# A new hand-written order for the first two batches of a fused attention and feed-forward kernel

## The chip, the cores and the metric

The kernel runs on one core of a Trainium2 chip. The metric is the device time of one execution in microseconds (us). In the text PE is the matrix engine, DVE the vector engine, ACT the activation engine, POOL the general engine that also issues "software" DMAs, SP the engine that only issues DMAs. PEld is PE's weight load. Each engine works through its own list in order and waits on semaphores for the others.

## The reference

Cosine attention over 8 batches of 12 heads (448 positions, 64 wide), then a two-layer feed-forward net with exact gelu on the 3584 tokens:

```
q_n = q / (norm(q) + 1e-6);  k_n = k / (norm(k) + 1e-6)
attn = softmax(q_n @ k_n.T / tau)
x = (attn @ v) as (3584, 768)
out = gelu(x @ w_in) @ w_out        # w_in 768 x 2048, w_out 2048 x 768
```

Input and output are float32; the matrix products run in bfloat16.

## The kernel before

Four heads form a quad; a batch has three quads, so there are 24, numbered 0 to 23. Quad 0 is handled as two halves (units 0 and 1), every other quad as one unit (unit u is quad u - 1). For each unit: Q and K are loaded (`load_qk`, SP's queue), squared (`square`) and summed (`reduce`, DVE), the norm is made as exp(0.5 ln) on ACT (`logs`, `roots`) and inverted on DVE (`inverses`), Q and K are multiplied by it (`scale`), transposed (`transposes`: on PE through a PSUM bank and a DVE copy, `copies`, or by a DMA on SP's queue). The first argument of `transposes`, `copies`, `scale`, `square` and `reduce` is a unit, that of `scores`, `exps`, `sums`, `values` and `normalise` a quad. `scores` writes a pair of PSUM banks, of which there are two (st0, st1), `exps` is one ACT instruction over such a pair. `sums` and `values` are products with ones and with V, `turned`, `inverted`, `spread` and `normalise` (DVE) divide by the sums and write x.

The feed-forward part of a batch: 96 products `mm` for 16 blocks of 128 columns (`hp`), a gelu for each (ACT), then "pieces" of the second layer (`op`), each of 16 steps `run(1)` of four instructions over 64x64 tiles; a piece ends in a reduce on DVE, or a copy on ACT and an add on DVE. The pieces of a batch run in the next batch's attention; two pairs of banks serve them in turn.

V and both weights are loaded by POOL (`load_v`, `load_wi`, `load_wo`), converted to bfloat16 on the way. W_in comes in four parts, W_out in four; `load_wi(3)` holds the upper half of the columns for the last third of x.

The first two batches are written out as a list in the function `opening()`; the place of a call in this list is the place of its instructions in its engine's own list. From batch 2's feed-forward on, loops (`attention`, `first`) make the order. Q and K live in four buffers in turn (`qkp`). `spin` is an idle product on constants, to keep PE busy at the start. `table` loads ACT's function table: one set has exp and logarithm, the other gelu. Norm inputs that are ready together share one `logs` and `roots`: the list `groups` says which units; each has a constant tile (`root2`) for its root:

```
groups = [[n] for n in range(NQ + 2)] + [[NQ + 2, NQ + 3], [2 * NQ + 1], [2 * NQ + 2]]
sr_t[n] = root2[2 if len(groups[n]) == 2 else n % 2][:, :math.prod(shapes[n])]
```

Of the kernel before, what the change touches and what calls it, by code (L numbers as in the profile page):

```python
# [9 lines left out]
F32 = mybir.dt.float32  # L10
# [6 lines left out]
def kernel(  # L17
# [73 lines left out]
    root2 += [consts.tile([128, 8 * C, 2], F32, name=f"root4_{n}") for n in range(1)]  # L91
    for t in root2:
        nc.vector.memset(t[:, :, 1], 1e-6)
# [33 lines left out]
    def load_qk(g, queue=None):  # L127
        b, n = divmod(g, NQ)
        t = qkp.tile([128, 2, 2, C, D], F32, tag="qk", name=f"qk{g}")
        qk_t[g] = t  # L130
        for s0, s1 in ((0, 1), (1, 2)) if g == 0 else ((0, 2),):
            for i, src in enumerate((q, k)):
# [4 lines left out]
                        "(s h) (p c) d -> (h p) s (c d)", h=2, c=C))  # L137

# [341 lines left out]
    def upto(f, n, last=None):  # L480
        last = {load_qk: NG, load_v: NV, root: len(groups), load_wi: NQ + 1, load_wo: 4}.get(f, NU)
# [56 lines left out]
    def opening():  # L538
        load_qk(0)
        table(EXP_SET)  # L540
        load_qk(1)
        load_qk(2)
        spin(20)
        late_copy()
        load_qk(3)
        x_t[0] = xp.tile([128, KD, S], BF16, tag="x", name="x0")
        square(0, ((AC, Q),))
        square(0, ((AC, K),))
        reduce(0, Q)
        reduce(0, K)  # L550
        square(1, ((AC, Q),))
        load_v(0)
        logs(0)
        reduce(1, Q)
        roots(0)
        load_wi(0)
        square(1, ((AC, K),))
        inverses(0)
        square(2, ((AC, Q),))
        reduce(1, K)  # L560
        scale(0, ((GP, 1),))
        logs(1)
        reduce(2, Q)
        roots(1)
        scale(0, ((GP, 0),))
        spin(2)
        transposes(0, 1)
        square(2, ((AC, K),))
        inverses(1)
        spin(1)  # L570
        transposes(0, 0)
        square(3, ((AC, Q),))
        copies(0, 1)
        scale(1, ((GP, 0),))
        copies(0, 0)
        square(3, ((AC, K),))
        scale(1, ((GP, 1),))
        load_qk(4)
        spin(1)
        transposes(1, 0)  # L580
        reduce(2, K)
        scores(0, ((0, 0), (0, 1)))
        load_v(1)
        transposes(1, 1)
        copies(1, 0)
        logs(2)
        scores(0, ((0, 2), (0, 3)))
        roots(2)
        load_wi(1)
        exps(0, ((0, 0), (0, 1)))  # L590
# [638 lines left out]
    def attention(b, fill):  # L1229
# [12 lines left out]
        def inverted_norms():  # L1242
            if 2 * b + 6 < len(groups):
                inverses(2 * b + 6)
# [191 lines left out]
```

## Time and profile before

| | |
|---|---|
| median of 3 runs | 391.37 us (391.14 to 391.41) |
| profiled execution, span of its instructions | 390.6 us |
| PE busy | 382.6 us (98%) |
| DVE, ACT, POOL busy | 273.0, 269.9, 248.7 us |
| DMA, mean rate | 140 GB/s |

In a list by engine, a row gives the start in us from the span's start, the length in us, engine, line of the program, operation, tile written and tiles read, shapes, how many instructions are merged, and in brackets the idle time before it with what ended it. "L267" is line 267. A row of a group gives busy time, mean length in ns, and idle time before. Line numbers of the profile are those of the kernel before; in the changed kernel most of them are 8 higher (L267 is L275 there, L427 is L435), those in its first part 1 to 4.

### The profile page before, as it was taken

How to read it: one execution, taken by the hardware profiler on the slowest of the kernel's cores; microseconds unless marked ns; L12 is line 12 of the kernel's file. 1: busy time of each engine (PE TensorE's matmuls, PEld its weight loads, DVE VectorE, ACT ScalarE, POOL GpSimd, SP SyncE). 2: the span in 40 equal slices, each digit the busy share in tenths (PEclk: the TensorE clock that was granted, in tenths of full speed). 3: DMA queues.
4: the chain of work that ended last, by engine and by line, in shares of the span. 5: the costliest groups of instructions: out<-in, count | busy, mean ns of one | idle time of the engine just before them, and what ended most of it. 6: DMA issues, size and time to landing. Idle time of an engine off the chain costs nothing.

```text
span 390.6 us, 13166 instructions
## 1 busy us (share of the span) xinstructions
PE 382.6 (98%) x5820; PEld 236.6 (61%) x5820; DVE 273.0 (70%) x509; ACT 269.9 (69%) x391; POOL 248.7 (64%) x161
## 2 busy tenths in 40 slices
PE   7899999999999999999999999999999999999996
PEld 3444568555777656865567556775567555655674
DVE  4878439876778896879696896889685993670032
ACT  5895789857999958996678767997577646504300
POOL 4796950557998399969594794969595770910000
PEclk9999999999999999999999999999999999999999
DMA  8999999926899691889067490876045600130033
GB/s 265 264 262 229 176 191 329 254 56 157 179 203 299 112 217 69 185 158 275 5 172 130 120 243 2 185 131 118 3 91 81 154 9 2 44 82 2 7 79 83
DMA packets 64473, 54.85 MB, mean 140 GB/s; under 512 B 38688, under 2 KB 60320, under 8 KB 64416
## 3 DMA queue, kind: packets, MB, share of 16 engines
q1 hardware_dynamic: 54464, 41.79, 42.0%
q0 software_dynamic: 9568, 11.80, 18.5%
q8 instruction: 45, 0.74, 0.8%
q10 hardware_dynamic: 384, 0.43, 0.4%
q14 instruction: 12, 0.10, 0.1%
HBM read 45.61 MB, written 11.01 MB: 145 GB/s over the span
## 4 chain that ended last, share of the span: by engine, by line
PE 95%; DMA 2%; SPq 1%; ACT 1%; issue 0%; DVE 0%; ACTq 0%
PE hp L493 37%; PE op L427 36%; PE st L257 9%; PE o L346 8%; DMA qk<-in_k_dram 2%; PE op L451 1%; PE sm L323 1%; PE sm L332 1%; PE tp L236 1%; SPq L134 1%; ACT sq L173 0%; ACT pt L267 0%; PE spin L489 0%; DVE last L454 0%; ACT root L195 0%
## 5 line engine op out<-in xcount | busy, mean ns | idle before, releaser
L427 PE MATMUL op<-wo,g 64*64 64x384 bf16 x3456 | 167.1, 323 | 0.2 <-issue 0.2
L267 ACT ACTIVATE pt<-st 128x896 bf16<-128x896 f32 x168 | 147.2, 918 | 19.6 <-PE st L257 17.5
L493 PE MATMUL hp<-x,wi 128*128 128x448 bf16 x768 | 147.0, 353 | 0.0
L427 PEld LDWEIGHTS <-g 64*64 64x64 bf16 x3456 | 106.2, 107 | 40.9 <-issue 4.2
L493 PEld LDWEIGHTS <-wi 128*128 128x128 bf16 x768 | 74.3, 98 | 71.6 <-issue 3.2
L219 POOL TENSOR_TENSOR qkb<-qk,rn 128x896 bf16<-128x896 f32 (+1 forms) x49 | 80.4, 1662 | 46.0 <-DVE rn L203 37.9
L278 POOL TENSOR_TENSOR acc<-acc,pt 128x896 f32<-128x896 f32 x55 | 103.8, 1888 | 4.3
L436 DVE TENSOR_REDUCE ot<-op 128x384 f32<-128x768 f32 x50 | 47.3, 946 | 54.7 <-PE op L427 47.5
L1357 ACT ACTIVATE g<-hp 128x448 bf16<-128x448 f32 x96 | 46.2, 547 | 55.1 <-PE hp L493 55.1
L257 PE MATMUL st<-qkT 64*64 64x448 bf16 x672 | 62.8, 352 | 0.5 <-ACT pt L267 0.5
L183 DVE TENSOR_REDUCE nq<-sq 128x14 f32<-128x896 f32 (+1 forms) x50 | 50.4, 1036 | 13.6 <-ACT sq L173 7.1
L380 DVE TENSOR_TENSOR x<-o,rs 128x448 bf16<-128x448 f32 x48 | 27.6, 611 | 22.9 <-PE o L346 21.9
L175 POOL TENSOR_TENSOR sq<-qk 128x896 f32<-128x896 f32 x16 | 26.6, 1685 | 23.8 <-DMA qk<-in_q_dram 13.3
L346 PE MATMUL o<-pt,v 64*64 64x448 bf16 x672 | 39.5, 349 | 0.0
L290 DVE TENSOR_TENSOR acc<-acc,pt 128x896 f32<-128x896 f32 x30 | 33.0, 1099 | 1.0
L173 ACT ACTIVATE sq<-qk 128x896 f32<-128x896 f32 (+1 forms) x33 | 28.8, 901 | 4.4 <-DMA qk<-in_q_dram 3.2
L257 PEld LDWEIGHTS <-qkT 64*64 64x64 bf16 x672 | 23.1, 106 | 11.7 <-issue 3.7
L375 DVE STREAM_TRANSPOSE rs<-rc 128x448 f32<-128x448 f32 x48 | 28.1, 621 | 0.4
L278 POOL TENSOR_TENSOR acc<-pt 128x896 f32<-128x896 bf16 x11 | 20.7, 1878 | 10.9 <-ACT pt L267 10.9
L346 PEld LDWEIGHTS <-v 64*64 64x64 bf16 x672 | 21.1, 107 | 9.2 <-issue 0.2
L522 ACT ACTIVATE g<-hp 128x448 bf16<-128x448 f32 x32 | 15.4, 547 | 12.8 <-PE hp L493 12.7
L295 DVE TRANSPOSE_TENSOR_REDUCE sa<-acc 128x28 f32<-128x896 f32 x17 | 18.8, 1104 | 0.2
(54 smaller groups left out, 176.0 us busy)
## 6 DMA issues: line engine op xcount, KB each, us to landing
qk<-in_q_dram SPq DMA_DIRECT2D x23, 448.0 KB, 4.9
qk<-in_k_dram SPq DMA_DIRECT2D x23, 448.0 KB, 5.8
out_dram<-ot SPq DMA_DIRECT2D x48, 192.0 KB, 4.0
v<-in_v_dram POOLq DMA_DIRECT2D x6, 672.0 KB, 7.2
wo<-in_moe_w_out_dram POOLq DMA_DIRECT2D x4, 768.0 KB, 10.6
wi<-in_moe_w_in_dram POOLq DMA_DIRECT2D x4, 512.0 KB, 13.8
out_dram<-ot SPq DMA_DIRECT2D x12, 96.0 KB, 2.1
wi<-in_moe_w_in_dram POOLq DMA_DIRECT2D x4, 256.0 KB, 14.1
```

What stands on the lines that cost most here:

```text
L173: eng.activation(sq, t, AF.Square)
L183: nc.vector.tensor_reduce(nq_t[n][:, j, i], sq_t[g, i][:, s0:s1], mybir.AxisListType.X, ALU.add)
L219: eng.tensor_tensor(qkb[:, i, :, s0:s1].rearrange("p c s d -> p s c d"), t[:, i, s0:s1], rn[:, i].to_broadcast([128, s1 - s0, C, D]), ALU. ...
L257: nc.tensor.matmul(st[cols, n, :S], lhsT=qkT[rows, 1, c, cols], rhs=qkT[rows, 0, :, cols], start=True, stop=True, tile_position=(64 * s, 6 ...
L267: nc.scalar.activation(pt, st[:, :, :S], AF.Exp, scale=inv_tau)
L278: nc.gpsimd.tensor_tensor(acc_t[g], all_t[g][:, 0] if c == 1 else acc_t[g], all_t[g][:, c], ALU.add)
L290: nc.vector.tensor_tensor(acc_t[g], acc_t[g], all_t[g][:, c], ALU.add)
L346: nc.tensor.matmul(bank_t[g, h][cols, :S], lhsT=v_t[g][rows, s, c, :], rhs=pt_t[g, s, c][rows], start=(c == 0), stop=(c == C - 1), tile_po ...
L427: nc.tensor.matmul(ps[cols, r, :NH], lhsT=g_t[sb][rows, kf, t * 128 + 64 * c:t * 128 + 64 * (c + 1)], rhs=wo[rows, kf, ni * NH:(ni + 1) * NH],
L436: nc.vector.tensor_reduce(part, ps[:, :, :NH].rearrange("p r d -> p d r"), mybir.AxisListType.X, ALU.add)
L493: nc.tensor.matmul(t, lhsT=wi[:, kd, m * 128:(m + 1) * 128], rhs=x_t[b][:, kd, :], start=(kd == 0), stop=(kd == KD - 1))
L1357: nc.scalar.activation(g_t[sb][:, m, hf * S:(hf + 1) * S], hps.pop(m), AF.Gelu)
```

## The change

The list in `opening()` is replaced down to the end of batch 1's attention. Quad 0's K of the first half is now squared on DVE and its second half's Q on POOL; K of quad 0 (first half) and of quad 1, and Q of quads 2, 3 and 5 are scaled on DVE rather than POOL; quad 2's Q is squared on POOL and quad 3's Q on DVE. V of quads 1 and 2 is loaded ahead of V of quad 0, and both ahead of all of W_in. A buffer for quad 5 is taken early (`gate`, with a small write by POOL), so that quads 3 and 4 take the buffers of quads 0 and 1 and their loads wait until those have been scaled; quad 5's load goes out behind quad 4's. Units 5 and 6 no longer share one logarithm and root: unit 6 (quad 5) has its own group at the end of the list, number 19, with a constant tile of its own. In batch 1's attention the list has the 96 steps of the second layer of batch 0 as before, in the same order of pieces, with the scores of quads 3 to 5 in another order of columns and at other places among them. There are six idle `spin` products fewer. Later in the list `attend` calls are written as the two calls that it makes.

```diff
+    root2 += [consts.tile([128, 4 * C, 2], F32, name=f"root6_{n}") for n in range(1)]
...
+    groups[NQ + 2] = [NQ + 2]
+    NR = len(groups)
+    groups.append([NQ + 3])
...
-        t = qkp.tile([128, 2, 2, C, D], F32, tag="qk", name=f"qk{g}")
+        t = qk_t[g] if g in qk_t else qkp.tile([128, 2, 2, C, D], F32, tag="qk", name=f"qk{g}")
...
+    def gate(g):
+        qk_t[g] = qkp.tile([128, 2, 2, C, D], F32, tag="qk", name=f"qk{g}")
+        nc.gpsimd.memset(qk_t[g][:, :, 0, 0, 0:1], 0.0)
...
-        sr_t[n] = root2[2 if len(groups[n]) == 2 else n % 2][:, :math.prod(shapes[n])]
+        sr_t[n] = root2[3 if n == NR else 2 if len(groups[n]) == 2 else n % 2][:, :math.prod(shapes[n])]
...
     def opening():
         load_qk(0)
-        table(EXP_SET)
-        load_qk(1)
-        load_qk(2)
-        spin(20)
-        late_copy()
-        load_qk(3)
...
+        square(0, ((DV, K),))
         square(0, ((AC, Q),))
         reduce(0, Q)
         reduce(0, K)
+        table(EXP_SET)
+        logs(0)
+        gate(5)
+        roots(0)
+        banks(1, 2, 0)
+        square(1, ((GP, Q),))
+        reduce(1, Q)
+        inverses(0)
+        load_v(1)
+        scale(0, ((GP, Q),))
+        square(1, ((AC, K),))
...
+        scale(0, ((DV, K),))
+        spin(20)
+        load_qk(1)
...
+        load_qk(2)
...
+        load_qk(3)
...
+        load_qk(4)
+        load_qk(5)
...
+        transposes(4, 0)
+        transposes(4, 1)
+        copies(4, 0)
+        run(1)
+        copies(4, 1)
+        gelu(0, 6)
+        inverses(19)
+        scale(6, ((DV, Q),))
+        run(1)
+        run(1)
+        scale(6, ((GP, K),))
+        scores(3, ((0, 0), (1, 0)), 0)
+        table(EXP_SET)
+        exps(3, ((0, 0), (1, 0)))
+        run(1)
+        run(1)
+        scores(3, ((0, 1), (1, 1)), 1)
...
+        spread(4, 1)
+        normalise(4, 1)
+        spread(4, 0)
...
+        normalise(4, 0)
+        run(1, AC)
+        banks(1, 4, 3)
+        values(5, (0,), p=2)
         sums(5, p=0)
```

Three places in the engines' own lists follow. ACT at the very start; sq is a square, lq a logarithm, root its root, pt an exponential, and the number behind the name is the quad (for lq and root the group). Before:

```order
L501 ACT_TABLE_LOAD
L173 ACTIVATE sq0_0_172<-qk0_133 128x448
L190 ACTIVATE lq0_182<-nq0_176,tiny_121 128x14
L173 ACTIVATE sq1_0_194<-qk1_139 128x896
L190 ACTIVATE lq1_199<-nq1_184,tiny_121 128x14
L173 ACTIVATE sq1_1_217<-qk1_139 128x896
L173 ACTIVATE sq2_0_233<-qk2_142 128x896
L173 ACTIVATE sq2_1_238<-qk2_142 128x896
L190 ACTIVATE lq2_271<-nq2_201,tiny_121 128x28
L267 ACTIVATE pt0_281<-st0_0_255 128x2x448
```

Now:

```order
L181 ACT_TABLE_LOAD
L181 ACTIVATE sq0_0_142<-qk0_135 128x448
L509 ACT_TABLE_LOAD
L198 ACTIVATE lq0_148<-nq0_144,tiny_121 128x14
L198 ACTIVATE lq1_167<-nq1_155,tiny_121 128x14
L181 ACTIVATE sq1_0_203<-qk1_192 128x896
L181 ACTIVATE sq1_1_205<-qk1_192 128x896
L275 ACTIVATE pt0_239<-st0_2_234 128x2x448
L275 ACTIVATE pt0_239<-st0_0_241 128x2x448
L198 ACTIVATE lq2_276<-nq2_260,tiny_121 128x28
L275 ACTIVATE pt0_239<-st0_4_288 128x2x448
L181 ACTIVATE sq2_1_312<-qk2_200 128x896
```

Two exponentials moved ahead of group 2's logarithm and of quad 2's square; a second table load came in behind the first square.

PE at the end of batch 0's first layer and the start of the second layer; tp4 is the transpose of quad 3, op a piece, st3 the scores of quad 3. One row stands for a run of equal ones. Before (the transposes stand 24 products ahead of these rows):

```order
L493 MATMUL hp0_13_817<-x0_171,wi_131 128x448
L427 MATMUL op0_0_0_829<-wo_132,g0_123 64x384
L257 MATMUL st3_0_894<-qkT3_754 64x448
L257 MATMUL st3_1_899<-qkT3_754 64x448
L427 MATMUL op0_1_0_921<-wo_132,g0_123 64x384
L257 MATMUL st3_2_945<-qkT3_754 64x448
L257 MATMUL st3_3_972<-qkT3_754 64x448
```

Now:

```order
L244 MATMUL tp4_0_815<-ident_108,qkb3_787 128x128
L244 MATMUL tp4_1_823<-ident_108,qkb3_787 128x128
L435 MATMUL op0_0_0_832<-wo_134,g0_123 64x384
L265 MATMUL st3_0_855<-qkT3_814 64x448
L265 MATMUL st3_1_871<-qkT3_814 64x448
L265 MATMUL st3_2_884<-qkT3_814 64x448
L265 MATMUL st3_5_907<-qkT3_814 64x448
L265 MATMUL st3_6_920<-qkT3_814 64x448
L435 MATMUL op0_1_0_942<-wo_134,g0_123 64x384
```

Before, 12 steps of the first piece stand ahead of st3_0, which st3_1 follows at once, and st3_2 comes four steps into the second piece. Now three steps stand ahead of st3_0 and 2, 2, 3 and 2 steps between the five groups, all in the first piece.

DVE at the end of batch 1's attention; rs is `spread`, the row that writes x is `normalise`. Before:

```order
L375 STREAM_TRANSPOSE rs4_0_1482<-rc4_1433 128x448
L375 STREAM_TRANSPOSE rs4_1_1492<-rc4_1433 128x448
L380 TENSOR_TENSOR x1_1089<-o4_1452,rs4_0_1482 128x448
L380 TENSOR_TENSOR x1_1089<-o4_1452,rs4_1_1492 128x448
L354 STREAM_TRANSPOSE tr5_1539<-sm5_1520 128x448
```

Now:

```order
L383 STREAM_TRANSPOSE rs4_1_1485<-rc4_1473 128x448
L388 TENSOR_TENSOR x1_301<-o4_1421,rs4_1_1485 128x448
L383 STREAM_TRANSPOSE rs4_0_1488<-rc4_1473 128x448
L388 TENSOR_TENSOR x1_301<-o4_1421,rs4_0_1488 128x448
L442 TENSOR_TENSOR ot0_2_1073<-ot0_2_1073,op0_2_1_1398 128x384
L362 STREAM_TRANSPOSE tr5_1569<-sm5_1540 128x448
```

Each half of quad 4 is now normalised right behind its own spread, and a piece's add stands ahead of quad 5's sums.

More of the change, by code (lines that the diff above doesn't have):

```diff
@@ L579, in opening @@
-        spin(1)
-        transposes(1, 0)
+        table(EXP_SET)
[9 more added lines that the diff above has]
+        square(1, ((AC, K),))
+        reduce(1, K)
+        logs(1)
+        roots(1)
+        scale(0, ((DV, K),))
+        spin(20)
+        load_qk(1)
+        bank(0, 12)
+        inverses(1)
+        load_qk(2)
+        square(2, ((AC, Q),))
@@ L581, in opening @@
+        square(2, ((AC, K),))
+        transposes(0, 0)
+        copies(0, 0)
+        load_qk(3)
+        transposes(0, 1)
+        copies(0, 1)
+        load_qk(4)
+        load_qk(5)
+        scores(0, ((0, 2), (0, 3)))
+        exps(0, ((0, 2), (0, 3)))
+        scores(0, ((0, 0), (0, 1)))
+        scale(1, ((GP, Q),))
+        transposes(1, 0)
+        scale(1, ((GP, K),))
+        late_copy()
+        load_v(0)
+        reduce(2, Q)
+        banks(0, 2, 0)
         reduce(2, K)
-        scores(0, ((0, 0), (0, 1)))
@@ L583, in opening @@
-        load_v(1)
+        bank_o(0, 15)
         transposes(1, 1)
         copies(1, 0)
+        exps(0, ((0, 0), (0, 1)))
+        copies(1, 1)
         logs(2)
-        scores(0, ((0, 2), (0, 3)))
         roots(2)
-        load_wi(1)
-        exps(0, ((0, 0), (0, 1)))
+        bank(0, 10)
+        banks(0, 0, 1)
+        bank(0, 11)
         inverses(2)
-        copies(1, 1)
-        exps(0, ((0, 2), (0, 3)))
-        spin(2)
+        square(3, ((GP, Q),))
         scores(0, ((0, 4), (0, 5)))
-        scale(2, ((GP, 0),))
@@ L649, in opening @@
+        scores(1, ((0, 6), (1, 6)))
+        normalise(0, 0)
+        exps(1, ((0, 6), (1, 6)))
+        transposes(3, 1)
         scores(1, ((0, 4), (1, 4)))
-        values(0, (6,))
-        spread(0, 0)
+        copies(3, 1)
         sums(1, (0,))
-        square(4, ((GP, K),))
         exps(1, ((0, 4), (1, 4)))
         sums(1, (1,))
-        scores(1, ((0, 5), (1, 5)))
-        normalise(0, 0)
-        transposes(3, 1)
-        exps(1, ((0, 5), (1, 5)))
-        scores(1, ((0, 6), (1, 6)))
@@ L706, in opening @@
[L706 removed]
         values(2, (3,))
         values(2, (4,))
[L709 removed]
+        bank(0, 13)
+        sums(2, (3,))
+        sums(2, (4,))
         exps(2, ((0, 6), (1, 6)))
[L711 to L719 removed]
         sums(2, (5,))
         sums(2, (6,))
[L722 removed]
+        turned(1)
@@ L774, in opening @@
         roots(5)
+        mm(0, 5, 0, 6)
+        table(GELU_SET)
+        gelu(0, 5)
+        mm(0, 1, 4, 6)
+        mm(0, 3, 4, 6)
+        mm(0, 4, 4, 6)
+        mm(0, 15, 0, 6)
+        gelu(0, 1)
+        gelu(0, 4)
+        mm(0, 14, 0, 6)
+        mm(0, 2, 4, 6)
+        gelu(0, 14)
+        mm(0, 0, 4, 6)
+        mm(0, 10, 0, 6)
+        gelu(0, 2)
+        gelu(0, 15)
+        gelu(0, 0)
+        gelu(0, 3)
+        gelu(0, 10)
+        reduce(4, Q)
+        open_third()
+        mm(0, 12, 0, 6)
@@ L1361, in first @@
             nc.scalar.preload_act_table_set(EXP_SET)
-            due = [n for n in range(done.get(root, 0), 2 * b + 8) if n < len(groups)]
+            due = [n for n in range(done.get(root, 0), 2 * b + 8) if n < NR]
             for n in due:
@@ L1365, in first @@
                 roots(n)
-            done[root] = max(done.get(root, 0), min(2 * b + 8, len(groups)))
+            done[root] = max(done.get(root, 0), min(2 * b + 8, NR))
             owed.extend(due)
```

543 lines of the change are left out of this document (266 added, 277 removed).

## The prediction

> **What bounds the kernel now.** I read the page first (busy shares, the slices), then the list of waits of PE, then the timeline engine by engine up to 92 us, where the rows that the change moves end.
>
> ```profile
> span 390.6 us, 13166 instructions
> PE 382.6 (98%) x5820; PEld 236.6 (61%) x5820; DVE 273.0 (70%) x509; ACT 269.9 (69%) x391; POOL 248.7 (64%) x161
> DMA  8999999926899691889067490876045600130033
> ```
> ```profile
> PE spin L489 <- DVE root L93: 1.9, 1, 1.9
> PE spin L489 <- DVE qkT L241: 0.9, 1, 0.9
> PE tp L236 <- POOL qkb L219: 0.6, 2, 0.4
> PE st L257 <- ACT pt L267: 0.5, 1, 0.5
> ```
>
> PE is the bound: all its waits come to about 4 us and all lie ahead of 15 us. Every PE instruction kept costs the same afterwards, and there are only six fewer, idle spins. So the change can win only by starting the real work earlier, and lose by making PE wait where today it does not. The DMA slices say what may stop it: the 16 engines are full (9) over nearly the first 70 us.
>
> **The opening: a head start of about 1.7 us.** The rows that set it, on PE, DVE, POOL and ACT:
>
> ```profile
> 12.36 0.57 PE L257 MATMUL st<-qkT 64*64 64x448 bf16 x4
> ...
> 7.14 0.24 DVE L203 RECIPROCAL rn<-se 128x14 f32<-128x14 f32 x1
> 10.70 1.08 DVE L241 COPY qkT<-tp 64x896 bf16<-64x896 bf16 x2
> ...
> 7.86 1.86 POOL L219 TENSOR_TENSOR qkb<-qk,rn 128x448 bf16<-128x448 f32 x2
> ...
> 12.66 0.95 ACT L173 ACTIVATE sq<-qk 128x896 f32<-128x896 f32 x1 [0.97 <-DMA qk<-in_k_dram]
> 13.52 0.30 ACT L190 ACTIVATE lq<-nq,tiny 128x28 f32<-128x28 f32 x1
> 13.99 4.13 ACT L267 ACTIVATE pt<-st 128x896 bf16<-128x896 f32 x5
> 20.35 12.07 ACT L267 ACTIVATE pt<-st 128x896 bf16<-128x896 f32 x14 [0.16 <-PE st L257]
> ```
>
> Quads 0 to 2 are issued as early as before, so the first reciprocal stays at 7.4. Today POOL scales both halves in a row (7.86 + 1.86 = 9.7); now K goes to DVE, so both are there at about 9.0 (7.5 + 0.93, and half a microsecond for the two engines side by side, see POOL below). Two transposes and two copies (1.08) later, the first scores stand at about 10.7 instead of 12.36, and the first exponential at 11.15 instead of 13.99: ACT no longer squares quad 2 ahead of it, a square that waited 0.97 us for its data. From there to quad 1's first exponential ACT needs today 20.35 - 13.99 - 0.16 = 6.2 us (seven exponentials, one logarithm with its root); now a second such pair (13.52 to 13.99, 0.47) and a square (0.95) stand among them: 11.15 + 7.6 = 18.75. The 14 exponentials of quads 1 and 2 then take 12.07 as today: last one at 30.8, not 32.42. Bounds: nothing to 2.8 us (13.99 - 11.15); I take 1.6.
>
> **The weights take back 0.9 of it.** Software-queue issues on POOL, and their times to landing (second one of each row):
>
> ```profile
> 23.91 1.26 POOL L467 DMA_DIRECT2D wi<-in_moe_w_in_dram  x2
> 42.92 1.56 POOL L473 DMA_DIRECT2D wo<-in_moe_w_out_dram  x2
> ```
> ```profile
> wi<-in_moe_w_in_dram POOLq DMA_DIRECT2D x1, 256.0 KB, 14.5
> ...
> wo<-in_moe_w_out_dram POOLq DMA_DIRECT2D x1, 768.0 KB, 10.3
> ```
>
> The last of W_in lands at 24.55 + 14.5 = 39.0, the last of W_out at 43.7 + 10.3 = 54.0. The DMA is full and the bytes ahead of these are the same in either order (both halves of V, W_in; quads 3 to 5 on the other queue), so I keep both landings. Quad 3's load goes out some 7 us later, but today it queues behind quad 2, whose K is used at 12.66; it arrives at most about 1 us later. First-layer products and what follows them:
>
> ```profile
> 33.29 13.42 PE L493 MATMUL hp<-x,wi 128*128 128x448 bf16 x70
> 46.54 0.94 PE L236 MATMUL tp<-ident,qkb 128*128 128x128 bf16 x14
> ...
> 51.95 2.15 PE L427 MATMUL op<-wo,g 64*64 64x384 bf16 x48
> ```
>
> 70 products take 46.54 - 33.29 = 13.25, 0.189 each. Now PE starts them at about 31.1, has 36 of them (6.8) and two chunks of values (some 0.8 with the changes of tile shape) behind it at 38.7, and the 37th needs the last W_in: a wait of about 0.35 to 39.05. The 60 left take 11.36, the two transposes of quad 3, now behind all of them, 0.8 to 0.9: the second layer starts at 51.3 instead of 51.95. **Gain 0.65** (nothing, if the weights land 0.7 later; 1.0 if they are there).
>
> **The start of the second layer gives back 1.3.** Rows of this place today:
>
> ```profile
> 53.93 0.55 PE L257 MATMUL st<-qkT 64*64 64x448 bf16 x8
> 54.31 1.47 PE L427 MATMUL op<-wo,g 64*64 64x384 bf16 x32
> 55.61 0.36 PE L257 MATMUL st<-qkT 64*64 64x448 bf16 x4
> ...
> 47.13 1.15 DVE L241 COPY qkT<-tp 128x896 bf16<-128x896 bf16 x2 [2.89 <-PE tp L236]
> ...
> 52.62 1.28 ACT L501 ACT_TABLE_LOAD   x1
> 54.34 3.40 ACT L267 ACTIVATE pt<-st 128x896 bf16<-128x896 f32 x4 [0.43 <-PE st L257]
> ```
>
> A step of the second layer is four instructions: 32 take 55.61 - 54.31 = 1.30, so 0.1625 a step; a scores group 0.19. The two copies start 0.59 after the transposes (46.54 to 47.13) and take 1.15. Today they hide under 24 products. Now the transposes stand last, at 50.4, so the copies end at 52.15, and between stand only three steps, to 51.8: PE waits 0.4. Quad 3's first exponential starts 0.41 after its scores (53.93 to 54.34), and the exponential table is there only then too (gelu ends near 51.4, + 1.28): 52.7. The exponentials follow at 0.8 to 0.85 (3.40 for four, the last 0.92 long). Only two scores banks exist, and five scores groups stand among 12 steps, so each from the third waits for the exponential two before it: the third group would be due at 53.2 and gets its bank at 53.65 (0.4), the fourth due at 54.3, gets it at 54.45 (0.15), the fifth due at 55.0, gets it at 55.3 (0.3). **Sum of the four waits 1.3.** The 13th step starts at 55.5; today 12 steps and two scores groups are done at 54.31, which with three more groups would be 54.9. PE is 0.6 behind. Bounds: 0.4 (the copies alone) to 1.7 (each copy and bank a tenth later).
>
> **The end of the second batch adds the rest.** DVE frees what PE ends on:
>
> ```profile
> 55.25 0.96 DVE L436 TENSOR_REDUCE ot<-op 128x384 f32<-128x768 f32 x1 [6.96 <-ACT pt L267]
> 71.78 0.65 DVE L354 STREAM_TRANSPOSE tr<-sm 128x448 f32<-128x448 f32 x1 [1.19 <-PE sm L332]
> 75.04 1.12 DVE L380 TENSOR_TENSOR x<-o,rs 128x448 bf16<-128x448 f32 x2
> ...
> 75.30 0.85 PE L332 MATMUL sm<-pt,ones 128*32 128x448 bf16 x16
> 76.26 1.49 PE L346 MATMUL o<-pt,v 64*64 64x448 bf16 x28
> 77.69 2.63 PE L493 MATMUL hp<-x,wi 128*128 128x448 bf16 x13
> ```
>
> From the first output piece's reduce (55.25) to quad 4's last normalise (76.16) DVE is idle for 1.19 only; quad 5's values start at 76.26, right behind. Now the first piece ends 1.2 later (55.5 + four steps, against 54.31 + four), so the chain starts 1.2 later; the idle 1.19 absorbs that, and each half of quad 4 is spread and at once normalised, 0.1 to 0.2 each more: values at about 76.5. But one chunk of values now goes ahead of quad 5's sums and six behind: 0.19 + 0.78 + 1.13 and three changes of shape (0.1 each) to the first product of batch 1, 2.4, where today 77.69 - 76.26 = 1.43 follow: 78.9 against 77.69. **Sum: 1.2 + 0.3 - 1.2 + 0.95 = 1.25 us later.** By PE alone it would be 0.6.
>
> Quad 4's keys, transposed by DMA, may add to it:
>
> ```profile
> DMA to landing us min/median/max: 4.0/5.5/6.3
> ...
> 87.84 1.09 DVE L219 TENSOR_TENSOR qkb<-qk,rn 128x896 bf16<-128x896 f32 x1
> ...
> 87.89 5.09 POOL L219 TENSOR_TENSOR qkb<-qk,rn 128x896 bf16<-128x896 f32 x2 [0.38 <-DVE rn L203]
> ...
> L219 POOL TENSOR_TENSOR qkb<-qk,rn 128x896 bf16<-128x896 f32 (+1 forms) x49 | 80.4, 1662 | 46.0 <-DVE rn L203 37.9
> ```
>
> Behind quad 3's reciprocal (about 46.5, after the ninth gelu and the table) POOL has three scales and a V issue in a row, 5.8 us: 52.3. Beside DVE's scale two POOL scales took 5.09, 0.85 more each than the mean; DVE now scales quad 3's and quad 5's queries beside them: up to 54. Landing 4.0 to 6.3 later is 56.3 to 60.3; PE is there at 58.8. I take no wait; the end of the bounds is 1.5. The Trainium skill, "SBUF — State Buffer", section "SBUF: two separate sides", has DVE and GpSimd take one port pair in turn, whoever starts first holding it for its whole instruction. By it DVE's scale of quad 5 would stand behind POOL's instead, and POOL would be done near 53.1; the rows above show only POOL lengthened.
>
> A second table load stands in the opening, ahead of the first logarithm; it hides under two reduces and costs up to 0.1. The Trainium skill ("ScalarE: Activation LUTs", section "What ACT_TABLE_LOAD costs") gives about 2.66 us a switch, a drain included. By that the first logarithm would be 1.4 later. This trace shows no drain:
>
> ```profile
> 41.48 1.28 ACT L501 ACT_TABLE_LOAD   x1
> 42.77 0.34 ACT L190 ACTIVATE lq<-nq,tiny 128x56 f32<-128x56 f32 x1
> ```
>
> **Rivals.**
> *A, not slower: the DMA is freer.* With quad 3's load held back, the software queue has the engines to itself for about 1 us near 12.6. If the last W_in lands by 38.5, the wait of 0.35 goes; if the DMA transpose takes 4.0, nothing waits there either, and if batch 2's end goes by PE (0.6) and not by DVE, 0.6 - 0.35 is left: 391.6. It decides from a landing of 38.5. For it: W_in's issue rows stand close to the landing that binds. Against: the first W_in issue is 7 us later than today (two scales, a square and both V issues go ahead).
> *B: the weights are late.* If the software queue runs dry near 14 to 16 us, W_in lands 1.5 later, and 1.25 becomes 2.75: 394.1. It decides from 40.5. For it: the late issue; against: 672 KB of V are queued ahead.
> *C: no head start*, by whatever holds up the first logarithm or scale by over 1.6: 1.25 + 0.65 = 1.9: 393.3. For it: two engines now share the squares and scales; against: the 0.97 wait that goes is certain.
> *D: faster.* Head start kept at 1.0 and none of the four waits: about 390.5. It needs PE to find both copies and the scores banks free, for which nothing in the rows speaks.
>
> **How the numbers follow.** Forecast 0.45, A 0.30, B 0.10, C 0.08, D 0.07. The profiled execution has a span of 390.56 us; the runs' median is 391.37, 0.8 more around it, which stays. So 391.37 + 1.25 = 392.6. Its own range is 391.9 (PE alone, 0.6) to 393.5 (the late keys). With A and B the range is 391.1 to 394.0. A measurement of this kernel tells about 0.2%, 0.8 us, from no change: faster (under 390.6) 0.08, D and a little of A; same 0.28, most of A and the low end of the forecast; slower 0.64.
>
> **What would show it.** Right: first scores near 10.7, exponentials of quad 2 done near 30.8; second layer starting near 51.3; PE waits for the copies and for exponentials, about 1.3 in all, between 51 and 55.5, where the old list has none; first product of batch 1 near 78.9 instead of 77.69; nothing new behind it. Wrong: a first product of batch 1 before 78, PE waits there under 0.5, or W_in landing outside 38.5 to 40.5.

## The result, and the profile after

The changed kernel takes 395.34 us (median of 7 runs, 394.06 to 397.21) against 391.41 (391.14 to 393.22) of the kernel before: a ratio of 1.0099, 95% interval 1.008 to 1.0117. It is 3.9 us slower. The prediction had 392.6 with a range to 394.0: the sign is right, the size is a third. Five of the 67 later executions of the kernel before fell into a slower state (mean clock 0.98, 6 to 8 us longer) and are left out of the medians and ratios below.

From the page of the changed kernel, span, busy shares, DMA slices and the chain that ended last by engine:

```profile
span 393.1 us, 13162 instructions
PE 383.0 (97%) x5814; PEld 237.5 (60%) x5814; DVE 280.2 (71%) x519; ACT 269.3 (69%) x391; POOL 243.6 (62%) x158
DMA  8999999719799773779156590766044610130033
PE 83%; DMA 5%; DVE 4%; POOL 3%; ACT 3%; issue 1%; SPq 0%; POOLq 0%; DVEq 0%
```

PE has the same work (383.0 us, 382.6 before). But the chain, 95% PE before, is now 83% PE, with DMA, DVE and POOL in it. The list of waits of PE says what PE stands at (the first five rows; total, times, longest), and below it one row of the list before:

```profile
PE spin L497 <- DVE g L88: 2.0, 1, 2.0
PE st L265 <- DVE qkT L249: 1.5, 4, 0.8
PE op L435 <- issue: 0.9, 2, 0.7
PE tp L244 <- DVE qkb L227: 0.5, 1, 0.5
PE op L435 <- DVE ot L444: 0.5, 1, 0.5
```
```profile
PE op L427 <- issue: 0.2, 1, 0.2
```

The waits for DVE's copies (`qkT`) ahead of scores, for its scale (`qkb`) and for its reduce (`ot`) are new. "issue" is a wait for nothing that the profile shows; before there was one of 0.19, ending at 125.58; the row has 0.9 now. Three of the four waits for `qkT`, and the one for `qkb`, lie in the opening, ahead of 19 us. Where the others lie, in the timeline of PE (start, length, line, what; in brackets the idle time before):

```profile
50.88 0.68 PE L435 MATMUL op<-wo,g 64*64 64x384 bf16 x12
51.81 0.38 PE L265 MATMUL st<-qkT 64*64 64x448 bf16 x4 [0.24 <-DVE qkT L249]
...
53.21 0.38 PE L265 MATMUL st<-qkT 64*64 64x448 bf16 x4 [0.18 <-ACT pt L275]
...
55.02 1.50 PE L435 MATMUL op<-wo,g 64*64 64x384 bf16 x32
...
65.40 0.38 PE L265 MATMUL st<-qkT 64*64 64x448 bf16 x4
...
66.45 0.33 PE L435 MATMUL op<-wo,g 64*64 64x384 bf16 x3
67.48 1.94 PE L435 MATMUL op<-wo,g 64*64 64x384 bf16 x41 [0.70 <-issue]
...
79.73 18.33 PE L501 MATMUL hp<-x,wi 128*128 128x448 bf16 x96
132.61 18.33 PE L501 MATMUL hp<-x,wi 128*128 128x448 bf16 x96
```

The second layer starts at 50.88, the first product of batch 1 stands at 79.73, that of batch 2 at 132.61. From there to the end the profiles of the two kernels differ by 0.2 at most. At 65.40 PE takes up quad 5's scores. The timeline of POOL and of SP's queue, and for the two DMA transposes there the times from issue to landing:

```profile
50.85 4.21 POOL L227 TENSOR_TENSOR qkb<-qk,rn 128x896 bf16<-128x896 f32 x2
...
55.13 0.80 POOL L163 DMA_DIRECT2D v<-in_v_dram  x1
...
52.58 3.97 SPq L239 DMA_TRANSPOSE qkT<-qkb  x2
```
```profile
DMA to landing us min/median/max: 4.0/7.1/10.3
```

Quad 4's transpose takes 4.0 us. Quad 5's is issued at 55.09, when POOL ends the scale, and 0.04 us later POOL issues the rest of the batch's V: it takes 10.3, to 65.36.

The third place, in the chain of waits:

```profile
94.10 5.37 DMA qk<-in_q_dram
...
103.06 1.03 DVE nq L191
104.08 0.87 DVE ot L444
...
105.00 1.17 PE op L435 x24
```

A load of q ends late, the squares and reduces behind it too, and the reduce that frees a bank of the output pieces stands behind them on DVE.

### The profile page after: what moved, and what is told of

Read it like the earlier page. It is cut to its first block, busy times and chain, and to the rows that moved or that the text cites. A ratio compares the mean times of both kernels' runs of the same rounds, so it can differ in the third digit from the quotient of the medians.

```text
span 393.1 us, 13162 instructions
## 1 busy us (share of the span) xinstructions
PE 383.0 (97%) x5814; PEld 237.5 (60%) x5814; DVE 280.2 (71%) x519; ACT 269.3 (69%) x391; POOL 243.6 (62%) x158
## 4 chain that ended last, share of the span: by engine, by line
PE 83%; DMA 5%; DVE 4%; POOL 3%; ACT 3%; issue 1%; SPq 0%; POOLq 0%; DVEq 0%
PE op L435 32%; PE hp L501 32%; PE o L354 8%; PE st L265 7%; POOL qkb L227 3%; DMA qkT<-qkb 3%; DMA qk<-in_q_dram 2%; DVE nq L191 2%; PE op L459 1%; ACT L509 1%; ACT g L530 1%; PE sm L331 1%; DVE qkT L249 1%; PE sm L340 1%; DVE qkb L227 0%
## 5 line engine op out<-in xcount | busy, mean ns | idle before, releaser
L227 POOL TENSOR_TENSOR qkb<-qk,rn 128x896 bf16<-128x896 f32 (+1 forms) x44 | 75.4, 1732 | 49.4 <-DVE rn L211 41.3
L183 POOL TENSOR_TENSOR sq<-qk 128x896 f32<-128x896 f32 (+1 forms) x17 | 27.6, 1635 | 36.8 <-DMA qk<-in_q_dram 24.1
L265 PEld LDWEIGHTS <-qkT 64*64 64x64 bf16 x672 | 24.0, 106 | 15.1 <-DVE qkT L249 3.5
L181 ACT ACTIVATE sq<-qk 128x896 f32<-128x896 f32 (+1 forms) x30 | 26.8, 921 | 2.1 <-DMA qk<-in_q_dram 1.9
## 6 DMA issues: line engine op xcount, KB each, us to landing
wi<-in_moe_w_in_dram POOLq DMA_DIRECT2D x4, 512.0 KB, 10.3
```

The source lines that it names most:

```text
L227: eng.tensor_tensor(qkb[:, i, :, s0:s1].rearrange("p c s d -> p s c d"), t[:, i, s0:s1], rn[:, i].to_broadcast([128, s1 - s0, C, D]), ALU. ...
L265: nc.tensor.matmul(st[cols, n, :S], lhsT=qkT[rows, 1, c, cols], rhs=qkT[rows, 0, :, cols], start=True, stop=True, tile_position=(64 * s, 6 ...
```

## The experiments

Each kernel is told by its time, its ratio to the kernel before on the same chip (with 95% interval), and by legs of its profiled execution, read from PE's timeline: the start of the second layer, the second batch (from there to the first product of batch 1) and the third (from that to the first product of batch 2). The steps are as many in all. Legs are compared rather than spans, because in two of the profiles (marked *) the granted clock fell to half between 15 and 22 us, which makes the start 2 us later and leaves the legs alone. In one (marked **) it was half from 68.6 to 72.0, inside the second batch. A leg is that of one execution: the two profiles of the kernel before differ by 0.43 in the second batch, the two of the changed kernel by 0.55.

| kernel | median us, ratio (interval) | second layer from | second batch | third batch |
|---|---|---|---|---|
| before, profile of the prediction | 391.41 | 51.95 | 25.74 | 52.21 |
| before, again | 391.66, 1.0025 (0.9993 to 1.0056) | 50.35 | 26.17 | 52.08 |
| changed | 395.34, 1.0099 (1.008 to 1.0117) | 50.88 | 28.85 | 52.88 |
| changed, again | 394.62, 1.0107 (1.0061 to 1.0154) | 51.14 | 28.30 | 52.96 |
| V held | 393.41, 1.0058 (1.0039 to 1.0076) | 52.85* | 27.21 | 53.08 |
| third V early | 394.24, 1.0077 (1.0039 to 1.0116) | 51.14 | 28.03 | 52.02 |
| both V edits | 392.74, 1.0058 (1.0027 to 1.009) | 50.73 | 27.20 | 52.51 |
| opening only | 392.56, 1.0008 (0.9984 to 1.0031) | 51.17 | 26.70 | 51.71 |
| before, V not held | 396.40, 1.013 (1.0096 to 1.0163) | 52.37 | 28.61 | 52.10 |
| steps first | 395.51, 1.0101 (1.0067 to 1.0135) | 52.95* | 28.56 | 52.09 |
| three mended | 394.41, 1.0085 (1.0048 to 1.0123) | 51.02 | 28.63 | 52.58 |
| both V, respaced | 394.43, 1.0079 (1.0061 to 1.0097) | 50.89 | 30.10 | 51.71 |
| opening filled | 395.56, 1.0121 (1.0071 to 1.0172) | 51.18 | 31.87** | 53.70 |
| loads early | 395.61, 1.0108 (1.0087 to 1.0128) | 51.66 | 28.10 | 53.74 |

### The kernel before, again

> The kernel before itself, unchanged, as the yardstick: 391.4 us (390.8 to 393.2). It tells how much of the 3.9 us between the two medians is beside the 2.5 us between the two profiled spans. If the time around the span is a constant, about 1.8 us as in all seven runs of the changed kernel, the profiled span of before (390.56) belongs to an execution of about 392.3 and the runs at 391.4 have spans of about 389.6. If it is 0.8 us here, the changed kernel loses 1.0 us outside its span.

391.66 us; the profiled execution took 391.00 with a span of 389.2. The time lies 1.7 to 1.85 us above the span in every execution of every kernel here, so what lies around the span is a constant, and the execution that the prediction read (span 390.56) was one of about 392.3, 0.9 above its median. The new one is 0.4 below it. PE's timeline in the new profile:

```profile
50.35 2.14 PE L427 MATMUL op<-wo,g 64*64 64x384 bf16 x48
76.52 18.33 PE L493 MATMUL hp<-x,wi 128*128 128x448 bf16 x96
128.60 18.33 PE L493 MATMUL hp<-x,wi 128*128 128x448 bf16 x96
```

The second layer starts at 50.35, not 51.95. What differs is how long the loads of quads 1 and 2 took (five issues from 1.7 to 3.7 us), first in the profile of the prediction, then in this one:

```profile
DMA to landing us min/median/max: 3.9/6.9/8.9
```
```profile
DMA to landing us min/median/max: 3.7/5.5/7.0
```

Quad 2's K came 1.9 us earlier, and ACT waited 0.42 for it instead of 0.97; the first exponentials then start at 12.39 (13.99 in the other profile):

```profile
10.77 0.95 ACT L173 ACTIVATE sq<-qk 128x896 f32<-128x896 f32 x1 [0.42 <-DMA qk<-in_k_dram]
...
12.39 3.32 ACT L267 ACTIVATE pt<-st 128x896 bf16<-128x896 f32 x4
```

So against this execution the changed kernel starts its second layer 0.53 later, not 1.07 earlier, loses 2.68 in the second batch and 0.80 in the third: 4.0 in all, with 3.9 between the spans. That the medians too are 3.9 apart is in part chance. Five of the twelve executions of the changed kernel (both sets) show a mean clock of 0.987 to 0.991; 6.8 us at half clock in a span of 394, as in one profile below, make 0.991. The six at 0.997 and above have a median of 394.5, the 52 of the kernel before beside the experiments one of 391.5: 3.0 apart. By the mean of the two profiles of each kernel the start is 0.1 earlier, the second batch 2.6 longer, the third 0.8 longer: 3.3.

The earlier first scores (10.25) bring no earlier second layer. ACT's rows, of the changed kernel and then of the kernel before, show where the head start goes:

```profile
10.86 1.73 ACT L275 ACTIVATE pt<-st 128x896 bf16<-128x896 f32 x2 [0.63 <-PE st L265]
...
13.75 0.94 ACT L181 ACTIVATE sq<-qk 128x896 f32<-128x896 f32 x1
...
18.85 11.61 ACT L275 ACTIVATE pt<-st 128x896 bf16<-128x896 f32 x14 [0.26 <-PE st L265]
```
```profile
18.75 12.07 ACT L267 ACTIVATE pt<-st 128x896 bf16<-128x896 f32 x14 [0.16 <-PE st L257]
```

The first exponential is 1.53 earlier (10.86 against 12.39), but the square and one more logarithm with its root now stand behind it, and ACT works without a break to 18.59: quad 1's first exponential is 0.10 later. The 14 exponentials end 0.36 earlier (30.46 against 30.82), but PE has 20 products with V (1.12) behind its last scores that it had ahead of them before.

### V held behind quad 5's keys

```diff
-        nc.gpsimd.tensor_copy(then, all_t[g][:, c, 0, 0:1])
+        nc.gpsimd.tensor_copy(then, qkT_t[NQ + 2][:, 1, c, 0:1])
```

> The changed kernel, with the rest of the second batch's V held on POOL until quad 5's transposed keys have landed, and not until an exp. Theory, transfers: the V load is issued 0.04 us behind quad 5's DMA transpose and shares the engines with it, so the transpose takes 10.27 us; PE loses about 0.5 us ahead of quad 5's scores and about 0.9 us where it waits for nothing but its own instructions, whose load came late. With V held the transpose takes at most 6.5 us, the issue wait of 0.70 us near 66.8 goes, and the time falls by 1.2 us to about 394.0. Rival, order: the new order of the second batch costs by itself (changes of tile shape, waits for exps); the transpose may get shorter, but the time stays above 394.9. If V then lands behind 73 us, PE waits there for values of quad 4, and the time rises.

393.41 us, ratio 1.0058 where the changed kernel has 1.0099. The transposes take 3.5 and 4.8 us:

```profile
DMA to landing us min/median/max: 3.5/4.2/4.8
```
```profile
61.94 0.33 POOL L169 COPY then<-qkT 128x1 bf16<-128x1 bf16 x1 [4.91 <-DMA qkT<-qkb]
62.21 0.80 POOL L163 DMA_DIRECT2D v<-in_v_dram  x1
```

PE's issue wait near 67 is gone, and the second batch takes 27.21 instead of 28.85: 1.64 less (1.09 less than in the repeat of the changed kernel below). Of the 1.64, 0.31 stood ahead of quad 5's keys, 0.90 at the issue wait, 0.44 at the issue wait of 0.22 near 73.7. The transfers theory holds: nothing else was moved, and the loads of Q and K that run there too stayed. V lands at 72.65, and PE does not wait for it.

### The third batch's V early

```diff
         square(8, ((GP, Q),))
+        load_v(3)
         square(7, ((GP, K),))
...
         square(9, ((GP, K),))
-        load_v(3)
```

> The changed kernel, with the third batch's V load issued on POOL behind the second of six squares, as in the kernel before, and not behind the sixth. Theory: the PE wait of 0.45 us at 104.5 and the 0.65 us that are lost between 80 and 107 us come from that load, which lands at 95.5 among quad 6's transpose and q load and makes them 0.7 and 0.9 us longer than in the kernel before; with it early the wait goes and the time falls by 0.6 us to about 394.7. Rival: the second loss only follows from the first, PE being 2 us late; then the wait stays and the time is 395.3 within 0.3.

394.24 us, in an interval as wide as the effect. The trace is clearer: V lands at 82.06, not 95.54; the q load behind takes 3.90 instead of 5.37, quad 6's transpose 3.45 instead of 4.70; DVE's reduce is in time, PE's wait at 104.5 is gone, and the third leg is 52.02 instead of 52.88. One reservation: the kernel with twelve steps first left this load where it was and does not have that wait either (leg 52.09), with PE 1.8 us later at that place. So the order alone does not bring the wait; how late the loads are by PE's own progress decides, and V among them is one way to make them late.

In this profile quad 4's keys were the late ones (6.2 us):

```profile
PE st L265 <- DMA qkT<-qkb: 0.4, 1, 0.4
```

### Both V edits

> The changed kernel with two edits, both of V loads: the second batch's rest held behind quad 5's keys, the third batch's issued behind the second square. Theory: the two losses stand apart and add up, 1.6 and 0.8 us off 394.6: about 392.2, with the second batch at 27.2 us from its first step to the first product, and 52.0 us from there to the third batch's first product. Rival: as in the kernel with three edits the time stays at 394 or above, because a wait of PE for VectorE (a bank not yet read) comes up in place of each.

392.74 us, 1.9 less than the repeat of the changed kernel (394.62) and 2.6 less than its first median; the legs are 27.20 and 52.51, of which 0.50 is an issue wait at 125.8. The ratio is no lower than with V held alone (1.0058 both), because two of the five executions have a clock of 0.991. At 0.997 and above the medians are 394.5 (changed, six executions), 393.9 (third V early, three), 393.4 (V held, eleven) and 392.7 (both, three): 0.7 and 1.2 alone, 1.8 together (the kernel before has 391.3 to 391.6 on the chips of the experiments). By these and the legs the two losses are separate, on few executions. What stands then against the kernel before is mainly the start of the second layer, whose four losses are there as in the changed kernel.

### The opening alone

The changed list to the last gelu of batch 0, then the second batch as in the kernel before:

```diff
-        run(1)
+        run(3)
         copies(4, 1)
...
+        run(4)
         scores(3, ((0, 0), (1, 0)), 0)
+        scores(3, ((0, 1), (1, 1)), 1)
+        run(8)
         exps(3, ((0, 0), (1, 0)))
...
+        behind(3, 1)
+        rest_v()
```

> The opening of the changed kernel up to the start of the second layer, its later loads and quad 5's own root, and behind it the second batch in the order of the kernel before (twelve steps of the output pieces ahead of the first scores). Theory: the opening wins the 1.07 us by which the second layer starts earlier, and all of the loss sits in the new order of the second batch: about 390.4. Rival: the loss comes with the opening, because quad 5's scale ends only at 55.1 and its transpose meets V whatever the order: 391.4 or above, with a transpose of 8 us or more and an issue wait of PE near 66.

392.56 us, ratio 1.0008: no difference from the kernel before can be told. The second batch's order holds most of the loss (26.70 instead of 28.85), so that half of the theory stands. The 1.07 us that the opening was to win are not there: they were a difference to one slow opening. Quad 5's transpose took 7.6 here, with V issued 1.0 us behind it and not 0.04, and PE had issue waits of 0.21 near 65 and 0.33 near 72: the rival's sign, the first at a third of its size.

### The kernel before, V not held

```diff
         transposes(5)
+        rest_v()
...
-        behind(3, 1)
-        rest_v()
```

> The kernel before, with the rest of the second batch's V issued on POOL right behind quad 4's second scale, so beside both DMA transposes, and not held until an exp (55.6 to 57.2 us there). Theory, transfers: the two transposes, 6.3 to 6.6 and 5.5 us today, take 8 us or more, quad 4's keys land at 58.5 or later and quad 5's at 61 or later, the qk loads behind them on SP's queue land later too; since the order of before needs these keys only from about 63 us on, it costs little, 0 to 0.8 us: 391.5 to 392.3. Rival: a transpose is long for another reason than V beside it; then both stay under 7 us.

396.40 us: much more than expected. Both transposes are long, as the theory has it (6.3 and 5.5 in the kernel before):

```profile
DMA to landing us min/median/max: 7.9/8.7/9.5
```

PE never waits for their keys. It waits for its own instructions, in the old order, at 61.0, 67.5 and 74.6:

```profile
PE op L427 <- issue: 2.2, 3, 1.0
PE o L346 <- DMA v<-in_v_dram: 2.0, 1, 2.0
```

The second batch takes 28.61, 2.4 us more than in the repeat of the kernel before. In this profile PE also waits 2.0 at 25.4 for the first batch's V, which the edit does not touch and which was in none of the other profiles. Against 391.6 for the kernel before on this chip, the fastest of the five executions (394.72) loses 3.1 and the median 4.8, so 0.7 to 2.4 us are not explained by the second batch. The price of the edit was misjudged because a late key was the only harm thought of.

### What an issue wait is

The trace has the packets of the instruction queue (the page's "q8 instruction: 45, 0.74" MB, 16 KB each): 45 loads for some 11,630 products and weight loads, so about 256 of these PE instructions a load. Counting them places the waits: all 19 issue waits of 0.19 us or more behind 16 us, in 11 of the 14 profiles, stand at the same instruction of a block. PE has begun 256k and 193 or 194 instructions (k is 4, 5, 6 or 13), and it goes on 1.2 to 1.6 us after load number k has ended. So load k brings what follows there, and PE stands because it is not there yet. How late is a load? For each profile, PE instructions begun when load k started, less 256k, against the issue wait of PE 1 to 3 us later (a few records can be missing):

```
late by      issue waits in us, of the first 14 loads of every profile
up to 100    0 to 0.05
102 to 110   0, 0, 0.09, 0.19, 0.21, 0.22 (four times), 0.25, 0.30
             (before, 13th load: 0.19; changed, 6th and 13th: 0.22 and 0.21; changed again, 5th: 0.30)
118 to 126   0.21, 0.33, 0.33, 0.43, 0.50, 0.52, 0.53
             (both V, 13th: 0.50; before with V not held, 6th: 0.33)
132 to 138   0.65, 0.70, 0.94, 0.98
             (V held, 13th: 0.65; changed, 5th: 0.70; before with V not held, 5th and 4th: 0.94 and 0.98)
154          hidden behind a wait for quad 5's keys (opening filled, 5th)
```

The later a load starts by PE's own count, the longer PE stands: the issue wait is PE out of instructions. Whether the transfers hold the load back was tested from both sides. The load near 60 to 67 us is late by 102 to 154 in six of the eight profiles in which V runs beside quad 5's transpose (78 and 79 in the other two), and by 46 to 87 in the four in which V is held; the kernel before has 60 and 90. So V makes this load later, but not in every execution. For the waits near 128 us, which come with and without the edits, no cause was tested. The Trainium skill, "Runtime: NRT & Kernel Launch", section "Instruction fetch mechanics", has each engine fetch blocks of 256 instructions over a DMA queue of its own, and calls the cost of a block "mostly hidden". The 16 KB loads agree; the cost here was up to 0.98 us for one block.

### Twelve steps first, and the three edits together

```diff
+        run(5)
         scale(6, ((GP, K),))
+        open_fourth()
+        run(6)
         scores(3, ((0, 0), (1, 0)), 0)
+        scores(3, ((0, 1), (1, 1)), 1)
...
+        run(6)
         scores(3, ((0, 2), (1, 2)), 0)
...
+        run(5)
         scores(3, ((0, 5), (1, 5)), 1)
```

> The changed kernel, with twelve steps of the output pieces ahead of quad 3's first scores (three in the changed kernel) and four to six between the next scores, and nothing else moved. Theory: the 1.24 us that PE spends on more than its steps between 50.9 and 55.0 go, of them waits for the copies of quad 3 and for the exps; the time falls by 1.0 to 1.2 us to about 393.7. Rival: the transpose of quad 5 at 65.4 is the limit that follows and takes them back; then PE's wait at 65 grows from 0.1 to about 1.2 us and the time stays at 394.6.

> The changed kernel with all three edits: twelve steps first, the second batch's V held behind quad 5's keys, the third batch's V behind the second square. Theory: the losses stand apart and add up: 1.2, 1.6 and 0.8 us less, 391.0 to 391.6, level with the kernel before (the second batch takes 26.0 to 26.3 us from the first step to the first product, 26.17 in the kernel before; 28.85 in the changed kernel), and the 0.5 us of the opening is what is left. Rival: they share one cause and overlap, 392.5 or above.

395.51 and 394.41 us. Contrary to the expectation, the edit moves more than steps: the exponentials of quad 3 come earlier in ACT's list, and the step whose piece ACT ends (`run(1, AC)`) stands elsewhere. The waits between 50.9 and 55 are gone in both, but the second batch keeps 28.56 and 28.63. With the three edits PE waits at two new places:

```profile
PE st L265 <- ACT pt L275: 1.0, 2, 0.8
PE sm L340 <- DVE ot L444: 1.0, 1, 1.0
```

The first is the edit's own fault: quad 3's last and quad 4's first scores came to stand side by side, ahead of the exponentials that free their banks (0.76 and 0.26 us near 58 to 60). The second is DVE, which reads a bank late. Neither is the rival as written, but the times are nearer to the rivals'.

### Respaced by what an exponential takes

> The changed kernel with the two edits of the V loads, and quad 3's scores spaced by what the exps take (0.92 us each): six steps ahead of the first, three ahead of the next two, five between the others. Theory: the 1.24 us of waits between 50.9 and 55.0 go for the most part, so that 0.7 to 1.1 us less are left than with the two edits alone: about 391.3. Rival: what is won there is lost behind it, where VectorE reads the banks of the output pieces late; then PE waits for its reduce near 70 to 72 us, as in the two kernels with twelve steps first, and the time is that with the two edits or above.

394.43 us, 1.7 above the kernel with the two V edits. The start is clean, and PE loses more behind it:

```profile
PE op L435 <- DVE ot L442: 1.6, 1, 1.6
PE sm L340 <- DVE ot L444: 1.2, 1, 1.2
PE op L435 <- DMA wo<-in_moe_w_out_dram: 0.7, 1, 0.7
```

All five executions of this kernel are at full clock; those of the kernel with both V edits at full clock have 392.7. The rival holds: with PE's steps earlier, the last W_out is late for the 13th step (0.7), and DVE, whose reduces stand in its list behind sums that wait for exponentials, frees the banks 1.6 and 1.2 us late. The 1.24 us at the start can't be had by this spacing alone; DVE's list would have to be moved with it, which was not tried.

### Idle products in the opening

```diff
+        fill(4)
         scores(0, ((0, 2), (0, 3)))
...
-        spin(1)
+        fill(3)
         scores(0, ((1, 0), (1, 1)))
```

and the same at quad 1's third pair; `fill` writes a bank of `sm`.

> The changed kernel, with eight idle products more on TensorE where it waits between 9 and 15 us (four ahead of the first scores, two more at each of two places); their results are not read. Theory, clock: executions with a mean clock of 0.99 come from PE's waits in the opening; filled, they fall from 1 in 4 to at most 1 in 12, the median falls by 0.5 us or more and executions at full clock keep 394.6. Rival: they come whatever PE does there; then still 2 or more of 12 show 0.99, and the median is that of the changed kernel within 0.3.

395.56 us. None of its five executions shows a mean clock of 0.99 (two have 0.995 and 0.996, and the profiled one of them fell to half clock only at 68.6); the other kernels with the new opening show 0.986 to 0.992 in 15 of 73, the kernel before in none of 67 (five of these are at 0.98). That settles nothing: at 15 in 73, five executions without one come about one time in three. The median did not fall. Its profile holds the strongest case of the transfers: quad 5's transpose took 12.9 us, and PE stood right at it:

```profile
68.35 0.39 PE L265 MATMUL st<-qkT 64*64 64x448 bf16 x4 [2.74 <-DMA qkT<-qkb]
```

### The loads of quads 3 to 5 not held back

```diff
-        gate(5)
```

> The changed kernel without the memset that holds a buffer for quad 5, so that the loads of quads 3 to 5 start as early as their buffers allow (quad 3's right behind quad 2's). Theory of the prediction: the later loads are what keeps W_in on time; without them the last W_in lands at 39 us or later (38.0 in the changed kernel) and PE waits 0.3 to 1 us at the first layer: 395 to 395.7. Rival: the loads' place does nothing for PE; W_in lands within 0.5 us of 38.0 and the time is that of the changed kernel.

395.61 us, as the changed kernel. The theory's landing is wrong: the last W_in lands at 37.5, earlier than the 38.0 with the loads held. But an earlier part of W_in landed at 32.26 (30.32 with the loads held), and PE stood 0.74 for it at 31.7:

```profile
PE hp L501 <- DMA wi<-in_moe_w_in_dram: 0.7, 1, 0.7
```

The rival holds: the loads' place decides which part of W_in binds, by some tenths, and is no cause of the 3.9 us.

### The changed kernel, again

> The changed kernel itself, unchanged, beside the three that follow: 395 us (394 to 397). Theory, clock: about one execution in four (10 of 38 so far with the new opening) shows a mean clock of 0.99, some 7 us at half clock behind 15 us, and is 2 us longer; the rest lies at 394.6. Theory, instructions: the issue wait of PE near 67 us returns in the new profile, at 0.5 to 1.0 us, with quad 5's transpose at 9.5 us or more; the second layer starts at 50.9 to 51.2 us and the second batch's first product at 79.2 to 79.8. Rival: the issue wait was a thing of one execution; then that product stands at 78.9.

394.62 us; the losses return. Quad 5's transpose takes 9.6, the issue wait is 0.30, less than expected (and 0.22 near 73), the wait for DVE's reduce at 104 now 1.05, the first product of batch 1 stands at 79.44. Their sizes change from one execution to the next, their places do not. At full clock the kernel spreads over 1.3 us (394.06 to 395.34); the executions up to 397.7 are those with a clock of 0.99.

## Why the prediction was wrong

**PE is the bound, and PE's waits decide: right.** In the profiles, all of the loss is PE time without work or in longer steps. One reading was incomplete: the waits do not "all lie ahead of 15 us". The list had a fifth row, the issue wait of 0.19, and with it the first sign of what came.

**The opening's head start and the gain of 0.65: wrong, by 0.5 to 1.2 us.** First scores (10.25, predicted 10.7), first exponential (10.86, 11.15), quad 1's first (18.85, 18.75) and quad 2's last (30.46, 30.8) came as worked out, and the second layer stood where the sum put it (50.88, predicted 51.3). The yardstick was wrong: in the execution that was read, quad 2's load was 1.9 us late, and "the 0.97 wait that goes is certain" was a wait of that execution. Two signs were on the page: the wait on a DMA in the opening, and a span plus a remainder. The step "the runs' median is 391.37, 0.8 more around it, which stays" took the profiled execution for a median one; the constant is 1.8. Without the slow loads quad 2's last exponential gains 0.36 and not 1.6, and the start of the second layer is 0.53 later against the second profile, 0.1 earlier by the mean of two; the opening alone gave a ratio of 1.0008 (0.9984 to 1.0031). Rival C, no head start, was the right picture of this part and got 0.08.

**The weights take back 0.9: the landing held within 1 us, the wait did not come.** The last W_in landed at 38.0 (39.0 predicted), the last W_out at 53.4 (54.0); the 37th product did not wait. In the repeat it did, 0.32. The second layer started at 50.88 instead of 51.3. Rival A had this right, and it was worth 0.4.

**The start of the second layer gives back 1.3: right.** Over 0.1625 a step and 0.19 a scores group, PE spends 0.46, 0.35, 0.13 and 0.30 more, 1.24 in all, ending at 55.02. The four come where they were forecast (copies, then three banks). The waits that the list names are smaller (0.24 and 0.18); the rest lies in stops too short for it and in longer steps. The repeat has the same four to within 0.02.

**The end of the second batch, 78.9 by DVE's chain: wrong mechanism, 0.8 short (1.25, counted from the start of the second layer).** DVE was not what values waited for. After 55.02 PE lost 0.31 ahead of quad 5's keys, 0.90 and 0.44 at two instruction loads, and 0.87 at changes of shape and short stalls; the second profile of the kernel before loses 1.05 in all there. The prediction's 0.95 for the order of the last values and sums would count only if values waited for DVE; on PE that order cost 0.25 and 0.13 (four values from 77.26 to 77.69, 24 from 78.47 to 79.73). The failed step is "Quad 4's keys, transposed by DMA, may add to it": it priced POOL's lateness and a landing of 4.0 to 6.3, and took the landing for a property of the transpose. Quad 4's keys were in time (4.0 us). Quad 5's were not priced; with a landing of 6.3 they would have been there at 61.4, well before 65.4. They took 10.3, because POOL's next instruction in the listing sends 448 KB of V beside them. The instructions of PE, which travel by DMA too, were not in the sum at all. With V held back, the second batch is 1.1 to 1.6 us shorter; sent early in the old order, V makes it 2.4 longer.

**DVE's chain after all.** The kernels in which PE's start was mended show it: DVE's reduces then stop PE for 1.0 to 2.8 us. The chain is real; in the changed kernel it is hidden behind PE's own delay. A sum of the losses along PE is no sum of what mending them brings.

**"Nothing new behind it": wrong, by 0.8.** The third batch's V stands behind six squares instead of two; the order shows that, and its DMA was not followed. Less the issue waits near 128 us, the third batch takes 51.7 to 52.1 in the four profiles of changed kernels with this V early, 52.4 to 53.3 in five with it late, and 52.1 in the sixth, in which PE was late itself.

**POOL beside DVE, and the table load.** POOL was done with quad 5's keys at 55.06 (predicted "up to 54"). DVE's scale and the chain of waits:

```profile
52.33 1.18 DVE L227 TENSOR_TENSOR qkb<-qk,rn 128x896 bf16<-128x896 f32 x1
```
```profile
4.99 1.28 ACT L509
...
6.29 0.32 ACT lq L198
...
52.51 2.56 POOL qkb L227
```

DVE started 0.18 ahead of POOL's second scale. Of the 4.21 us of POOL's two scales (50.85 to 55.06) the second took 2.56 and the first 1.65, so the second took 0.91 more; DVE had 1.00 of its 1.18 left. That agrees with the Trainium skill's rule ("SBUF — State Buffer", section "SBUF: two separate sides") that whoever starts first keeps the port pair for its whole instruction. The prediction let POOL be first when it worked out what the rule would give, and then set it aside; with DVE first, rule and rows say the same. For the table load the prediction's row was right: 1.28, and the logarithm 0.02 behind it, no drain.

**The sum.** Predicted: -0.65 + 1.9 + 0 = 1.25. Measured, by the mean of two profiles of each kernel: -0.1 + 2.6 + 0.8 = 3.3, against the second profile alone +0.53 + 2.68 + 0.80 = 4.0. So three terms failed: the gain of the opening was none, V and the instruction loads lengthened the second batch, and the third was put at nothing. What the half clock adds (3.0 at full clock, 3.9 between all medians) was not thought of. No rival had two new waits at once, and all of them kept the one yardstick.

## What to carry to other kernels

Before a gain is worked out from a profile, see whether the place it comes from was ordinary in that execution: a wait for a DMA in it, and a span whose remainder to the median differs from other kernels', are signs that it was not. Where a change makes two transfers fall together, look up what POOL's and SP's next instruction sends, price the slowdown of both, and remember that PE's own instructions come by DMA too. In the three orders tried here, taking PE's waits out moved the wait to DVE's list, which had not been moved with it.

## What was not expected of the hardware

The DMA transposes of quads 4 and 5 took 3.5 to 6.6 us as long as the rest of V (448 KB) was issued over 2 us behind them; with it 0.04 to 1.0 us behind (or, in the old order, 0.1 to 3 us ahead) they took 7.6 to 12.9.

PE ran out of instructions when a 16 KB load started more than about 100 PE instructions late by the count above: up to 0.98 us a block, each time at the same instruction of a block. The profile calls it "issue".

The clock can fall to half with no long wait of PE. In the kernel with V held, PE had been busy 5.09 of the 7 us ahead, with no wait over 0.8; stretches of that profile (PE, PEld, DVE, ACT, POOL, granted clock):

```profile
8.00:15.00 7.00, 5.09 (x51) 2.73 (x52) 6.76 (x13) 6.30 (x11) 6.04 (x9) 1.00 1.13 284
15.00:22.00 7.00, 7.00 (x48) 2.54 (x48) 4.91 (x8) 4.92 (x8) 4.95 (x4) 0.53 1.07 234
```

It cost that execution some 2 us. Nearly the same stretch stayed at full clock in another profile (PE busy 5.08 of 7 us with both V edits), so such waits do not force it. With the opening filled, the half clock came behind the wait of 2.74, for 3.4 us. The Trainium skill, "TensorE: Matmul & The Clock Gate", section "HAM oscillation — how this bites in real kernels", warns of idle gaps over about 3.4 us; here half clock also followed 2.74 in one go, and waits up to 0.8 with 1.9 us idle in 7.
